# Attention, gated convolution and mixer in one kernel: four operand tiles instead of two for the eight heads scored in fp32, loaded two heads ahead

## The chip, the cores and the metric

The kernel runs on one core of a Trainium2 chip. The metric is the device time of one execution in microseconds (us). A core has a matrix engine (TensorE, PE in the profile), three engines for elementwise work (VectorE, DVE; ScalarE, ACT; GpSimd, POOL) and a queue engine (SyncE, SP) that does little but issue DMA transfers. Each engine runs its own instructions in program order; semaphores make one wait for another. ACT can issue DMAs too, and here it issues a handful at the start.

## What is computed

Three stages follow each other: attention with a bias that decays along the sequence, a gated convolution block, and a mixer.

```python
# attention: batch 4, 8 heads, 576 positions, 64 values per head
scores = scale * np.matmul(q, k.transpose(0, 1, 3, 2))
cum = np.cumsum(np.maximum(s, 0.0), axis=-1)
bias = -(cum[:, :, :, None] - cum[:, :, None, :])
scores = np.where(causal, -1000000000.0, scores + np.minimum(bias, 0.0))
attn = softmax(scores)
x = np.matmul(attn, v)             # heads side by side: 512 values per position
# gated convolution: 512 -> 1024 -> 512
h = np.maximum(x @ w_in, 0.0)
conv_out = sum of h shifted by -1, 0, 1 times conv_w
x = h * sigmoid(conv_out) @ w_out
# mixer
u = x + mixing over positions by U @ V (rank 32)
out = u + np.maximum(u @ w_ch1, 0.0) @ w_ch2
```

## The kernel before, in words

**Attention.** There are 32 heads (4 batches of 8), taken one after the other by `att_head`, in pairs for the last rows and for the products with v. For a head, PE makes the scores in blocks of 128 query rows (`scores`, L693: blocks of 128, 256, 384 and 512 columns, named sc0 to sc3 behind the head's number) and, for a pair of heads, the last 64 rows of both (`scores4`, L709). DVE takes the maximum of each block with the mask (L654), ACT takes the exponentials into tiles P (L671), POOL multiplies them by the reciprocal of the row sums (L682), PE transposes them by a multiplication with `ident` (`transp`, L816, into pt), ACT copies the result to tiles th (L357), and PE multiplies those with v (`av`, L842). As each pair is done, ACT and POOL split its output x into a high and a low part (xh, xl), which the first product of the gated block (`m1_in`, L886, into h) takes. Those products do not hang on later heads, so they serve PE as work to fill in with.

**The eight fp32 heads.** The 24 later heads take their scores from operands that are split into two rounded parts (qkA and qkB). The first eight heads, `FS = range(8)`, take them in fp32 from one operand tile qkF: partitions 64 to 127 hold the head's q and k (288 KB from memory, L592), partitions 0 and 1 hold a row of ones or minus ones and the head's row of the running sum cc (2.2 KB each), and the rest of partitions 0 to 63 is zero. There are two such tiles, qkF_0 for even heads and qkF_1 for odd ones. DVE clears their lower half once (L455) and ACT issues the four DMAs of ones (L458). `prep4(h)` (L588 to L601) issues the head's q and k (L592) and the two rows of cc (L594 and L599; for heads 0 and 1 the second goes through ACT, L597). Heads 0 and 1 are loaded at the start; from head 2 on, `att_head(h)` asks for head h + 1. The tile is in use until the scores of the head two before, with the pair's last rows, are done. The two tiles are then taken over by qkA of heads 8 and 9, as they are two buffers of the same ring, "qkA".

**What else goes on in this stretch.** The weights of the gated block (w1, 16 pieces of 512 KB, L539) are loaded through two buffers and decoded by ACT (L513) and DVE (L520, L529), then rounded by ACT (L357) and reduced to the rest by DVE (L366). The first eight pieces belong to heads 0 to 7 and go to tiles w1h and w1l. The other eight go to the tile `ws` of 8192 columns, under the name w1o; before that, `ws` holds early data: the rounded cc in columns 0 to 1151 (rk) and the raw mask in columns 1152 to 1343.

**What sets the order.** The kernel records all its operations with a cost each, and a planner (`Plan.order`) then lists them for each engine: at each point it takes, of the operations whose inputs are ready by its costs, the one that was recorded first. An earlier load therefore changes the order on all engines. All loads stand in SP's one queue; an instruction there that waits holds up all behind it. Eight semaphores are handed out to the DMAs in turn, those that ACT issues included, so that a DMA is issued only after the DMA eight places before it in the plan's order has landed.

Of the kernel before, what the change touches and what calls it, by code (L numbers as in the profile page):

```python
# [8 lines left out]
F32 = mybir.dt.float32  # L9
# [9 lines left out]
B, H, S, D = 4, 8, 576, 64  # L19
# [8 lines left out]
FS = range(8)  # L28
# [26 lines left out]
def f32(ap):  # L55
    return ap.bitcast(F32)
# [256 lines left out]
def tile_attention_moe_mixer(  # L313
# [14 lines left out]
    nc = tc.nc  # L328
    plan = Plan(tc)


    def dve(n, fn, r, w, fast=False):
        far = st.get("late") and any(getattr(x, "pool", None) is banks for x in r)
        return plan.op("DVE", (155 if far else 70) + n * (0.52 if fast else 1.042), fn, r, w)
# [4 lines left out]
    def pool(n, fn, r, w, two=False, extra=125):  # L339
        return plan.op("POOL", ((280 if st.get("late") else 148) + n * 2.1) if two else (37 + n * 0.834 + extra), fn, r, w)  # L340

    def dma(nbytes, fn, r, w):
        return plan.op("SP", 640, fn, r, w, late=nbytes / 360)

    def dma_act(fn, r, w):

        return plan.op("ACT", 100, fn, r, w, late=1900)
# [24 lines left out]
    st = {}  # L372
# [12 lines left out]
    def ring(pool_, cls, count, shape, dtype, name, at={}):  # L385
        n = at[pool_, cls] = at.get((pool_, cls), -1) + 1
        return pool_.buf(f"{cls}{n % count}", shape, dtype, name)
# [17 lines left out]
    def one(pool_, name, shape, dtype):  # L405
        return pool_.buf(name, shape, dtype, name)
# [8 lines left out]
    def early(name, at, shape, dtype, rows=128):  # L415
        n = 1
        for x in shape:
            n *= x
        axes = " ".join("abc"[: len(shape)])

        def view(t):
            v = t[:rows, at : at + n]
            if dtype != F32:
                v = v.bitcast(dtype)
            return v.rearrange(f"p ({axes}) -> p {axes}", **dict(zip("abc", shape)))

        return Part(ws, view, name)
# [13 lines left out]
    sm4s = [one(ap, f"sm4_{i}", [128, 5], F32) for i in range(2)]  # L441


    cc = one(ap, "cc", [NH, S], F32)
    rk = early("rk", 0, (2, S), F32R, NH)
    qkFs = [ring(ap, "qkA", RINGS["qk"], [128, 2, S], F32, f"qkF_{i}") for i in range(2)]

    def cum():
        return cc()
# [14 lines left out]
    scan = dve(S, lambda: nc.vector.tensor_tensor_scan(cum(), cum(), cum(), 0.0, ALU.add, ALU.max), key, key)  # L464

    def behind(o, back=1):
        o.preds.add([x for x in plan.ops if x.eng == "PE"][-back])
# [20 lines left out]
    def clear(t):  # L488

        o = pool(2 * S, lambda: nc.gpsimd.memset(f32(t[0:64]), 0.0), [], [(t, "r"), (t, "q")], extra=0)  # L490
        behind(o)

    for t in p4s:
        o = pool(64, lambda t=t: nc.gpsimd.memset(t[:, S:640], 0.0), [], [(t, "pad")], extra=0)
# [88 lines left out]
    def p_tiles(g):  # L583
        return [ring(ap, f"P{i}_", RINGS["P"], [128, 128 * (i + 1)], F32, f"P{g}_{i}") for i in range(4)] + [
            p4s[g // 2 % 2]
        ]

    def prep4(h):  # L588

        t = qkFs[h % 2]  # L590
        a = slice(64 * (h % 2), 64 * (h % 2) + 64)
        dma(294912, lambda: nc.sync.dma_start(out=t[64:128], in_=qk[h // 2, a]), [], [(t, "q")])  # L592
        rows = dma(
            2304, lambda: nc.sync.dma_start(out=t[0:1, 1, :], in_=cum()[h : h + 1]), [cc], [(t, "r0")]  # L594
        )
        if h < 2:
            dma_act(lambda: nc.scalar.dma_start(out=t[1:2, 0, :], in_=cum()[h : h + 1]), [cc], [(t, "r1")])  # L597
        else:
            dma(2304, lambda: nc.sync.dma_start(out=t[1:2, 0, :], in_=cum()[h : h + 1]), [cc], [(t, "r1")])  # L599
        st.setdefault("first", rows)  # L600
        st[h] = dict(qk=[t], P=p_tiles(h), sm=sms[h % 2])  # L601

    def prep_v(h):

        vr = ring(ap, "vr", RINGS["vr"], [128, 2, 5, 64], F32, f"vr{h}")
        dma(327680, lambda: nc.sync.dma_start(out=vr(), in_=vP[h // 2]), [], [vr]).preds.add(st["first"])
        st["v", h // 2] = vr

    def prep(h):

        t1 = ring(ap, "t1", RINGS["qkh"], [128, 2, S], F32R, f"t1_{h}")
        t2 = ring(ap, "t2", RINGS["qkh"], [128, 2, S], F32R, f"t2_{h}")

        for c, (hi, lo) in enumerate(((t1, t2), (t2, t1))):

            def raw(c=c, lo=lo):
                return f32(lo[:, c, :])

            dma(294912, lambda c=c, raw=raw: nc.sync.dma_start(out=raw(), in_=qk[h // 2, :, c]), [], [(lo, c)]).slack = WIRE
            if h == len(FS):  # L620
                behind(plan.ops[-1], 25)
            hi_pool(lambda c=c, hi=hi: hi[:, c, :], raw, [(lo, c)], [(hi, c)], S)
            lo_dve(
                lambda c=c, lo=lo: lo[:, c, :],
                raw,
                lambda c=c, hi=hi: hi[:, c, :],
                [(lo, c), (hi, c)],
                [(lo, c)],
                S,
            )  # L630
        st["pair", h // 2] = (t1, t2)
# [676 lines left out]


    prep4(0)  # L1310
    prep4(1)
    prep_v(0)
    mraw = early("mraw", 2 * S, (192,), F32)
    dma(98304, lambda: nc.sync.dma_start(out=mraw(), in_=mask_d), [], [mraw])
    for c, n in ((0, 384), (512, 224)):
        o = pool(n, lambda c=c, n=n: nc.gpsimd.memset(mask[:, c : c + n], 0.0), [], [(mask, c)], extra=0)
# [17 lines left out]
    def att_head(h):  # L1334

        if h + 1 < NH:
            if h % 2 == 1:
                prep_v(h + 1)
            if h + 1 in FS:
                if h:  # L1340
                    prep4(h + 1)
            else:
                if h % 2 == 1:
                    prep(h + 1)
                place(h + 1)
        if h == 3:
            decay_parts()
            for t in qkBs:
                clear(t)
        for i in range(2):  # L1350
            if h < NH:
                scores(h, i)
        if h > 0:
            transp(h - 1, 0)
        if h < NH:
            scores(h, 2)
        if h > 0:
            transp(h - 1, 1)
            if h % 2 == 0:
                av(h - 2, 0)  # L1360
        if h < NH:
            scores(h, 3)
        if h > 0:
            transp(h - 1, 2)
            transp(h - 1, 3)
        if h < NH and h % 2 == 0:
            scores4(h)
        if h > 0 and h % 2 == 0:
            av(h - 2, 1)
# [133 lines left out]
    for g in range(2):  # L1503
        blk = (w2a, u1p)[g].buf(f"u{g}", [128, 2 * 7 * S], F32R, f"w2_{g}")
        for i in range(7):
            f = 7 * g + i
# [89 lines left out]
```

## Time and profile before

| what | value |
|---|---|
| time, median of 3 runs (lowest to highest) | 809.51 us (807.74 to 813.28) |
| time of the profiled execution | 810.78 us |
| span of the profiled execution, first to last instruction | 809.0 us |
| PE busy | 788.1 us (97%), 5300 instructions |
| DVE, ACT, POOL busy | 477.1 us (59%), 465.8 us (58%), 181.5 us (22%) |
| TensorE clock granted, mean | 0.998 of full speed |

How to read it: an engine's busy share is taken over the whole span, and this kernel has stages of different kinds. In the forty slices of the profile's page, PE stands at 5, 8 and 8 tenths in the first three (20 us each), where the eight fp32 heads are, and at 9 from the fourth on except for the last. The rows below are from that part, up to about 90 us, and from the summary of the rest.

### The profile page before, as it was taken

The page shows a single profiled execution, that of the slowest core. Times are in us where ns is not written, and L with a number is a line of the kernel's source. Part 1 is how long each engine was busy: PE and PEld are TensorE (multiplying, and loading weights), DVE is VectorE, ACT ScalarE, POOL GpSimd, SP SyncE. Part 2 cuts the span into 40 slices and gives each one's busy share as a digit, 9 for nine tenths or more (in the row PEclk, how much of TensorE's full clock was granted, in tenths as well). Part 3 has the DMA queues.
Part 4 walks back from the last instruction along what each step waited for, and adds up shares of the span by engine and source line. Part 5 has one row for each costly group of instructions (what it writes and reads, how often), then busy time and mean ns, then how long its engine had stood idle before and what let it go on. Part 6 is the DMA issues. An engine that isn't in the chain of part 4 may idle for free.

```text
span 809.0 us, 15163 instructions
## 1 busy us (share of the span) xinstructions
PE 788.1 (97%) x5300; PEld 707.1 (87%) x5300; DVE 477.1 (59%) x1152; ACT 465.8 (58%) x1176; POOL 181.5 (22%) x291
## 2 busy tenths in 40 slices
PE   5889999999999999999999999999999999999998
PEld 3557798999899998999999999999998888888888
DVE  5977897636855368547888967444566232323232
ACT  4878898858868488776767545444455222222221
POOL 2554464634446245241220000000000000000000
PEclk9999999999999999999999999999999999999999
DMA  6578655554454456130226356455588363636343
GB/s 166 176 207 227 188 142 151 138 135 106 149 136 108 105 131 188 35 111 1 103 68 225 121 162 210 148 180 183 168 261 275 92 207 92 204 96 191 110 130 93
DMA packets 66309, 119.69 MB, mean 148 GB/s; under 512 B 9396, under 2 KB 34868, under 8 KB 66232
## 3 DMA queue, kind: packets, MB, share of 16 engines
q1 hardware_dynamic: 66160, 118.70, 50.7%
q8 instruction: 42, 0.69, 0.3%
q14 instruction: 35, 0.29, 0.1%
q10 hardware_dynamic: 72, 0.01, 0.0%
HBM read 68.81 MB, written 28.90 MB: 121 GB/s over the span
## 4 chain that ended last, share of the span: by engine, by line
PE 88%; DVE 4%; ACT 3%; DMA 2%; issue 1%; POOL 0%; SPq 0%; DVEq 0%; POOLq 0%
PE my L1273 24%; PE ma_A L1173 16%; PE y L928 12%; PE h L886 11%; PE ma_S L1173 6%; PE sc L693 6%; PE pt L816 5%; PE av L842 5%; DMA qkA<-t 1%; PE tp L945 1%; PE t L964 1%; DVE sc L654 1%; DMA qkF<-cc 1%; PE mh L991 1%; DVE wf_w L529 1%
## 5 line engine op out<-in xcount | busy, mean ns | idle before, releaser
L1273 PE MATMUL my<-mh,w 128*128 128x512 f32 (+1 forms) x560 | 159.1, 368 | 0.0
L1173 PE MATMUL ma_A<-u,W 128*128 128x288 f32 x960 | 137.9, 295 | 0.0
L1173 PEld LDWEIGHTS ma_A<-u,W 128*128 128x128 f32 x960 | 131.4, 188 | 0.3
L1251 ACT ACTIVATE mh<-ml 128x512 fp32r<-128x512 f32 (+1 forms) x80 | 47.1, 589 | 136.8 <-DMA ml<-ch_d 76.0
L1273 PEld LDWEIGHTS my<-mh,w 128*128 128x128 f32 x560 | 101.6, 189 | 17.6
L1254 DVE SCALAR_TENSOR_TENSOR ml<-ml,mh 128x512 fp32r<-128x512 f32 (+1 forms) x80 | 50.5, 638 | 112.6 <-ACT mh L1251 112.6
L928 PE MATMUL y<-gh,w1o 128*128 128x288 f32 x512 | 113.9, 299 | 0.1
L1273 PE MATMUL my<-ml,w 128*128 128x512 f32 (+1 forms) x280 | 103.0, 368 | 0.0
L682 POOL TENSOR_SCALAR P<-P,sm 128x128 f32<-128x128 f32 (+3 forms) x128 | 73.2, 591 | 101.3 <-DVE sm L745 86.5
L654 DVE CUSTOM_DVE_ANT_0 sc<-sc,mask 128x128 f32<-128x128 f32 (+2 forms) x144 | 69.2, 497 | 33.8 <-PE sc L693 26.1
L928 PEld LDWEIGHTS y<-gh,w1o 128*128 128x128 f32 x512 | 85.4, 188 | 0.9 <-DVE c L907 0.3
L898 DVE SCALAR_TENSOR_TENSOR c<-h,cw,c 128x288 f32<-128x288 f32 x128 | 64.3, 512 | 30.9 <-ACT c L894 29.8
L886 PE MATMUL h<-xh,w1h 128*128 128x290 f32 x256 | 79.9, 312 | 0.1
L369 POOL TENSOR_TENSOR gl<-c,gh 128x288 fp32r<-128x288 f32 x64 | 53.7, 846 | 104.0 <-ACT gh L913 89.2
L886 PE MATMUL h<-xl,w1h 128*128 128x290 f32 x256 | 76.6, 299 | 0.0
L886 PE MATMUL h<-xh,w1l 128*128 128x290 f32 x256 | 76.4, 298 | 0.0
L1187 ACT COPY s<-ma_A 128x288 f32<-128x288 f32 x96 | 38.3, 401 | 64.7 <-PE ma_A L1173 56.1
L928 PE MATMUL y<-gl,w1o 128*128 128x288 f32 x256 | 75.2, 294 | 0.0
L671 ACT ACTIVATE P<-sc,sm 128x128 f32<-128x128 f32 (+3 forms) x128 | 67.8, 533 | 5.9 <-DVE sm L654 5.4
L357 ACT COPY th<-pt 128x384 f32<-128x384 f32 (+2 forms) x128 | 63.1, 494 | 9.9 <-PE pt L816 9.0
L816 PE MATMUL pt<-ident,P 128*128 128x128 f32 x320 | 59.7, 274 | 2.3 <-ACT h L892 1.3
L1273 PEld LDWEIGHTS my<-ml,w 128*128 128x128 f32 x280 | 52.8, 189 | 8.6
(135 smaller groups left out, 1527.8 us busy)
## 6 DMA issues: line engine op xcount, KB each, us to landing
ml<-ch_d SPq DMA_DIRECT2D x64, 256.0 KB
ch_d<-s SPq DMA_DIRECT2D x64, 144.0 KB
raw_w<-w_in SPq DMA_DIRECT2D x16, 512.0 KB
raw_w2a<-w_in SPq DMA_DIRECT2D x16, 512.0 KB
raw_w2b<-w_in SPq DMA_DIRECT2D x16, 512.0 KB
t<-qk_in SPq DMA_DIRECT2D x24, 288.0 KB
qkB<-t SPq DMA_DIRECT2D x24, 288.0 KB
qkA<-t SPq DMA_DIRECT2D x24, 288.0 KB
```

Source lines behind the costliest of these rows:

```text
L357: act(n, lambda: nc.scalar.copy(out(), src()), r, w)
L369: pool(n, lambda: nc.gpsimd.tensor_tensor(out(), src(), f32(hi()), ALU.subtract), r, w, two=True)
L654: lambda: nc.vector.tensor_tensor_reduce(out=ps[:rows, :w], in0=ps[:rows, :w], in1=mask[:rows, m0 : m0 + w], scale=-0.125, scalar=3.0e38 i ...
L671: lambda: nc.scalar.activation(out(), ps[:rows, :w], ACTF.Exp, bias=low(), scale=-1.0, accum_out=total()),
L682: lambda: nc.gpsimd.tensor_scalar(t[:, :w], t[:, :w], r(), 1.0, ALU.mult, ALU.mult),
L816: nc.tensor.transpose(pt[:, o + rows - 128 : o + rows], d["P"][i][:, 128 * j : 128 * j + 128], turn)
L886: nc.tensor.matmul(ps[:, :W], lhsT=ww, rhs=xx, start=kt + n == 0, stop=kt == KT - 1 and n == 2)
L898: lambda k=k: nc.vector.scalar_tensor_tensor(c(), hh[:, k : k + HS], cw[:, 3 * f + k : 3 * f + k + 1], c(), ALU.mult, ALU.add),
L928: nc.tensor.matmul(ps[:, :HS], lhsT=ww, rhs=xx(), start=f + n == 0, stop=f == NF1 - 1 and n == 2)
L1173: nc.tensor.matmul(ps[:, :HS], lhsT=ww, rhs=uu, start=first and k == 0, stop=k == 5, skip_group_check=True)
L1254: lambda: nc.vector.scalar_tensor_tensor(ml[:, :n], raw(), 0.0, f32(mh[:, :n]), ALU.max, ALU.subtract),
L1273: nc.tensor.matmul(ys[c][dt][:, :n], lhsT=ww, rhs=xx[:, :n], start=f + k == 0, stop=f == NF2 - 1 and k == 2)
```

## The change

Two more operand tiles, qkF_2 and qkF_3, are laid into columns 2048 to 3199 and 3200 to 4351 of `ws`, which has no other user there until w1o is written. Their lower halves are cleared by POOL (1152 columns of 64 partitions each), and their four rows of ones are loaded by four more DMAs in SP's queue, which the planner may place only after the first head's row of cc. `prep4(h)` takes tile h % 4. `att_head(h)` now asks for head h + 2, so heads 2 and 3 are asked for when head 0 and head 1 begin. Head 4 goes into qkF_0 again, head 7 into qkF_3. The last users of qkF_0 and qkF_1 are now heads 4 and 5, and w1o may be written only after the scores of heads 6 and 7.

```diff
--- before.py
+++ after.py
@@ -441,6 +441,7 @@
     sm4s = [one(ap, f"sm4_{i}", [128, 5], F32) for i in range(2)]
 
 
+    rows4 = []
     cc = one(ap, "cc", [NH, S], F32)
     rk = early("rk", 0, (2, S), F32R, NH)
     qkFs = [ring(ap, "qkA", RINGS["qk"], [128, 2, S], F32, f"qkF_{i}") for i in range(2)]
@@ -489,6 +490,17 @@
 
         o = pool(2 * S, lambda: nc.gpsimd.memset(f32(t[0:64]), 0.0), [], [(t, "r"), (t, "q")], extra=0)
         behind(o)
+
+    for n in range(2):
+        t = early(f"qkF_{2 + n}", 2048 + n * 2 * S, (2, S), F32)
+        low = early(f"qkF_{2 + n}z", 2048 + n * 2 * S, (2, S), F32, 64)
+        low.state = t.state
+        o = pool(2 * S, lambda low=low: nc.gpsimd.memset(low(), 0.0), [], [(t, "z"), (t, "r0"), (t, "r1")], extra=0)
+        o.preds.add(scan)
+        for i in range(2):
+            dma(2304, lambda t=t, i=i: nc.sync.dma_start(out=t[i : i + 1, i, :], in_=one_d[i, 0:1, 0, :]), [], [(t, "z")])
+            rows4.append(plan.ops[-1])
+        qkFs.append(t)
 
     for t in p4s:
         o = pool(64, lambda t=t: nc.gpsimd.memset(t[:, S:640], 0.0), [], [(t, "pad")], extra=0)
@@ -587,7 +599,7 @@
 
     def prep4(h):
 
-        t = qkFs[h % 2]
+        t = qkFs[h % 4]
         a = slice(64 * (h % 2), 64 * (h % 2) + 64)
         dma(294912, lambda: nc.sync.dma_start(out=t[64:128], in_=qk[h // 2, a]), [], [(t, "q")])
         rows = dma(
@@ -597,7 +609,10 @@
             dma_act(lambda: nc.scalar.dma_start(out=t[1:2, 0, :], in_=cum()[h : h + 1]), [cc], [(t, "r1")])
         else:
             dma(2304, lambda: nc.sync.dma_start(out=t[1:2, 0, :], in_=cum()[h : h + 1]), [cc], [(t, "r1")])
-        st.setdefault("first", rows)
+        if "first" not in st:
+            st["first"] = rows
+            for o in rows4:
+                o.preds.add(rows)
         st[h] = dict(qk=[t], P=p_tiles(h), sm=sms[h % 2])
 
     def prep_v(h):
@@ -1336,10 +1351,9 @@
         if h + 1 < NH:
             if h % 2 == 1:
                 prep_v(h + 1)
-            if h + 1 in FS:
-                if h:
-                    prep4(h + 1)
-            else:
+            if h + 2 in FS:
+                prep4(h + 2)
+            if h + 1 not in FS:
                 if h % 2 == 1:
                     prep(h + 1)
                 place(h + 1)
```

The planner makes another order of this for the first 580 or so of PE's 3842 rows, and the same one behind that. Three places, as the built programs have them. In the names, the last number only counts buffers; P0_1 is block 1 of head 0, pt0_1 its second group of transposes, sc2_0 the first block of scores of head 2; all of rk, the mask and the new operand tiles carry the name ws. Lines are those of each program.

SP's queue at the start, up to the first load of v, before:

```order
L451 DMA cc_108<-s_in 32x576
L592 DMA qkF_0_104<-qk_in 64x1152
L592 DMA qkF_1_129<-qk_in 64x1152
L1314 DMA ws_134<-mask_in 128x192
L594 DMA qkF_0_104<-cc_108 1x16x36
L594 DMA qkF_1_129<-cc_108 1x16x36
L606 DMA vr0_155<-vP_in 128x640
```

and of the change:

```order
L452 DMA cc_108<-s_in 32x576
L604 DMA qkF_0_104<-qk_in 64x1152
L604 DMA qkF_1_129<-qk_in 64x1152
L1329 DMA ws_134<-mask_in 128x192
L604 DMA ws_134<-qk_in 64x1152 x2
L606 DMA qkF_0_104<-cc_108 1x16x36
L606 DMA qkF_1_129<-cc_108 1x16x36
L606 DMA ws_134<-cc_108 1x16x36
L611 DMA ws_134<-cc_108 1x16x36
L606 DMA ws_134<-cc_108 1x16x36
L501 DMA ws_134<-one_in 1x576 x2
L621 DMA vr0_178<-vP_in 128x640
```

The q and k of heads 2 and 3 moved ahead of the rows of heads 0 and 1. By the eight semaphores, the second of them (head 3) is issued after the second of ACT's rows of ones has landed, and the row of head 0 behind it after q and k of head 1 have landed. Behind the rows of heads 0 and 1 stand five more small loads before the first v.

On PE, three blocks of head 2's scores (sc2_0 to sc2_2) moved from behind the second group of head 0's transposes (pt0_1) to ahead of it.

ACT's rows around its rounding of the fourth piece of w1 (w1h_3), before:

```order
L671 ACTIVATE P3_2_431,sm_1_199<-sc3_2_405,sm_1_199 128x384
L357 CAST w1h_3_440<-wf_w1_3_0_409 128x512
L357 COPY th2_2_446<-pt2_2_433 128x384
L671 ACTIVATE P3_3_451,sm_1_199<-sc3_3_423,sm_1_199 128x512
L357 COPY th2_3_462<-pt2_3_453 128x320
```

and of the change:

```order
L686 ACTIVATE P3_2_447,sm_1_202<-sc3_2_408,sm_1_202 128x384
L357 COPY th2_2_453<-pt2_2_439 128x384
L686 ACTIVATE P3_3_461,sm_1_202<-sc3_3_428,sm_1_202 128x512
L357 COPY th2_3_468<-pt2_3_455 128x320
L686 ACTIVATE P4_0_476,sm_0_164<-sc4_0_445,sm_0_164 128x128
L357 CAST w1h_3_482<-wf_w1_3_0_459 128x512
```

The rounding moved behind two copies of head 2's transposes and the first exponential of head 4.

SP's queue around the load of head 7, before:

```order
L539 DMA raw_w1_7_0_597<-w1_in 128x512
L606 DMA vr6_604<-vP_in 128x640
L539 DMA raw_w1_0_512_632<-w1_in 128x512
L592 DMA qkF_1_129<-qk_in 64x1152
L594 DMA qkF_1_129<-cc_108 1x16x36
L599 DMA qkF_1_129<-cc_108 1x16x36
```

and of the change:

```order
L551 DMA raw_w1_4_0_433<-w1_in 128x512
L477 DMA r_d_57<-ws_134 64x1x576 x2
L604 DMA ws_134<-qk_in 64x1152
L606 DMA ws_134<-cc_108 1x16x36
L611 DMA ws_134<-cc_108 1x16x36
L551 DMA raw_w1_5_0_492<-w1_in 128x512
```

Head 7's load moved from behind the ninth piece of w1 to behind the fifth.

## Rows read from the trace of the kernel before

**Rows 1.** Busy time by stretch: us, length, engines' busy time (instructions), PEclk, DMA, GB/s

```profile
10.00:92.00 82.00, 72.56 (x445) 47.54 (x444) 64.48 (x185) 68.18 (x192) 42.12 (x59) 0.98 0.72 203
92.00:200.00 108.00, 107.79 (x821) 97.67 (x820) 72.38 (x216) 85.98 (x249) 53.42 (x84) 1.00 0.56 138
200.00:700.00 500.00, 499.73 (x3480) 468.86 (x3479) 303.31 (x688) 285.93 (x692) 84.63 (x131) 1.00 0.48 145
```

**Rows 2.** Waits of PE in 0 to 120 us: us in total, times, longest

```profile
PE sc L693 <- DMA qkF<-cc: 7.5, 1, 7.5
PE sc L709 <- DMA qkF<-cc: 2.2, 1, 2.2
PE sc L693 <- ACT th L357: 1.5, 1, 1.5
PE pt L816 <- ACT h L892: 1.3, 1, 1.3
...
PE sc L693 <- DMA qkA<-t: 0.4, 1, 0.4
```

**Rows 3.** Timeline of the start: start us, us, engine, line, operation

```profile
1.19 1.21 SPq L592 DMA_DIRECT2D qkF<-qk_in  x2
1.20 0.64 POOL L1316 MEMSET mask<- 128x384 bf16 x2
...
2.44 0.58 SPq L1314 DMA_DIRECT2D ws<-mask_in  x1
...
4.98 1.22 SPq L594 DMA_DIRECT2D qkF<-cc  x2
...
6.55 0.35 SPq L606 DMA_DIRECT2D vr<-vP_in  x1
...
7.47 2.26 PE L693 MATMUL sc<-qkF 128*128 128x128 f32 x5 [7.47 <-DMA qkF<-cc]
```

**Rows 4.** Instructions on tile qkF in 0 to 7.6 us: duration min/median/max, first and last start

```profile
L458 ACTq DMA_DIRECT2D qkF<-one_in x4: 213/264/513, 2.1 to 3.8; - x4
...
L597 ACTq DMA_DIRECT2D qkF<-cc x2: 504/556/607, 5.3 to 6.6; - x2
```

**Rows 5.** Busy time by stretch, columns as in rows 1

```profile
2.00:6.00 4.00, 0.00 (x0) 0.00 (x0) 2.73 (x4) 0.00 (x0) 0.00 (x0) 1.00 0.80 184
86.90:90.40 3.50, 3.50 (x18) 2.46 (x16) 2.02 (x5) 3.14 (x9) 1.66 (x3) 0.51 1.04 241
7.50:11.90 4.40, 4.40 (x8) 2.21 (x8) 1.47 (x6) 2.58 (x7) 0.00 (x0) 1.00 0.84 231
```

**Rows 6.** Timeline of PE, 17 to 20 us

```profile
17.46 0.33 PE L816 MATMUL pt<-ident,p 128*128 128x128 f32 x1 [0.72 <-POOL p L682]
...
19.41 1.24 PE L693 MATMUL sc<-qkF 128*128 128x256 f32 x4
```

**Rows 7.** Timelines of PE, DVE and ACT around 57 us, with the idle time before

```profile
56.85 0.67 PE L709 MATMUL sc<-qkF 128*64 128x288 f32 x2 [2.24 <-DMA qkF<-cc]
...
57.56 0.47 DVE L654 CUSTOM_DVE_ANT_0 sc<-sc,mask 128x288 f32<-128x288 f32 x1 [2.55 <-PE sc L709]
...
58.26 0.59 ACT L357 COPY th<-pt 128x512 f32<-128x512 f32 x1 [2.31 <-PE pt L816]
```

**Rows 8.** Timelines of DVE and POOL, 26 to 34 us

```profile
26.83 0.86 DVE L529 SCALAR_TENSOR_TENSOR wf_w<-raw_w,wf_w 128x512 int32<-128x512 int32 x1
...
31.30 2.65 DVE L529 SCALAR_TENSOR_TENSOR wf_w<-raw_w,wf_w 128x512 int32<-128x512 int32 x1
...
32.20 1.20 POOL L369 TENSOR_TENSOR xl<-x,xh 128x576 fp32r<-128x576 f32 x1
```

**Rows 9.** Instructions on tile qkB in 25 to 40 us: duration, starts

```profile
L490 POOL MEMSET qkB<- x2: 1050/1188/1327, 29.9 to 31.2; 64x1152 f32 x2
```

**Rows 10.** First rounding into w1o (timeline of ACT), first product from it (timeline of PE)

```profile
73.52 0.62 ACT L357 CAST w1o<-wf_w 128x512 fp32r<-128x512 f32 x1
...
112.96 0.40 PE L928 MATMUL y<-gh,w1o 128*128 128x288 f32 x1
```

## The prediction

> **What bounds the kernel now.** I read the busy time by stretch first, then PE's waits, then the timelines at the places that they name. Behind 92 us PE is the bound: in the 608 us from 92 to 700 it is idle for 0.5 us [rows 1]. The order of the instructions is the same there with the change, so whatever PE gains or loses up to 92 us should reach the end unchanged. Ahead of that lie three things a load could touch: the start, where PE waits 7.47 us for the first head's row of cc [rows 2, 3]; the idle time from 10 to 92 us, 82.00 - 72.56 = 9.44 us [rows 1]; and a stretch of 3.5 us at a granted clock of 0.51, which is the lower of the two levels and costs 3.5 x 0.49 = 1.7 us [rows 5]. All that could ever be won is therefore 9.44 + 1.7 = 11.1 us of some 810, and the start can only get worse.
>
> Of the 9.44 us, little waits for an operand tile. The list of PE's waits has one of 2.2 us for a row of cc in a qkF tile, and one of 0.4 us for a qkA tile, which takes its place over from a qkF tile [rows 2]. The first is the load of head 7. It cannot start before qkF_1 is free, and it then stands behind big pieces of w1. At 56.85 us DVE had been idle for 2.55 us and ACT for 2.31 us until PE went on [rows 7], so no other engine would have held PE up in its place. The rest waits for ACT, DVE and POOL.
>
> **The change, term by term.**
>
> *The start: loss.* SP now issues q and k of heads 2 and 3 ahead of head 0's row. Head 2's fits into SP's gap, which runs from 3.02 (the end of the mask's issue) to 4.98 us [rows 3]. Head 3's must wait for ACT's second row of ones to land. When does that land? ACT's second issue of a cc row waits for the same row of ones: the two issues are 0.5 to 0.6 us each, yet the second starts at 6.6 us, over a microsecond after the first at 5.3 [rows 4]. So it lands at about 6.55 us. Head 3's issue takes 1.21 / 2 = 0.6 us, so head 0's row is issued at about 7.15 instead of 4.98 us: +2.2 us. By another way: the two loads are 590 KB more on the wire ahead of that row; at the 231 GB/s that the busy stretch behind the start shows [rows 5] that is 2.55 us. The two ways overlap and do not add; I take **+2.4 us**. The least is +1.6 us: the row also waits for head 1's q and k, as the first load of v does now, which starts at 6.55 us behind a gap of 0.35 us [rows 3], and 6.55 - 4.98 = 1.57. The most is +4.0 us: if the row of ones lands behind head 2's data too, 295 KB at the 184 GB/s of 2 to 6 us [rows 5] are 1.6 us more on top of 2.4.
>
> *Other work added at the start: nothing.* POOL clears two lower halves, 1.05 to 1.33 us each by the same clear of the qkB tiles [rows 9]. Its clear of the mask moves from 1.20 to about 3.6 us [rows 3], while DVE needs it only behind the first scores, at 8 us or later. In SP's queue three more rows of cc (0.61 us each) and two rows of ones (up to 0.51 us each, by those on ACT [rows 4]) stand ahead of the first v, which moves from 6.55 to about 7.15 + 5 x 0.61 + 2 x 0.51 = 11.2 us; `ident` comes about 0.4 us behind it, and two more rows of ones stand behind that. A load takes about 2.5 us from its issue until PE goes on (4.98 to 7.47 [rows 3]), so `ident` is there at 14 us. The first transposes stand just ahead of 17.46 us [rows 6] and move back with the start. Were that cover gone, PE would stand still at the transposes for as long as it is short. The writes to w1o now wait for heads 6 and 7 as well; the first is at 73.5 us and the first use of w1o at 113.0 us [rows 10], 39 us apart, so this costs nothing.
>
> *Filling the pipeline: gain.* PE waits 0.72 us for POOL's first big product at 17.46 us [rows 6]. Three blocks of head 2's scores now stand ahead of that place, and two blocks of such scores alone are 1.24 us [rows 6]. **-0.7 us** (0 at worst, if these blocks wait for ACT to free their PSUM banks).
>
> *Head 7's wait: gain.* Its load now stands behind the fifth piece of w1 instead of the ninth, and its tile is free when head 3 is done, not when head 5 is. **-2.2 us**, from rows 7, and 0 only if another wait stood there.
>
> *The qkA wait: gain.* qkF_0 and qkF_1 are done with at heads 4 and 5, two heads earlier. **-0.4 us** [rows 2].
>
> *Waits for ACT, DVE and POOL: open.* What is left is 9.44 - 0.72 - 2.24 - 0.4 = 6.1 us. The largest, 1.5 us for ACT's copy th [rows 2], comes from an accident: DVE's step of the w1 decode at 31.30 us takes 2.65 us where it took 0.86 us shortly before, beside a POOL instruction that ends at 33.40 us [rows 8], and ACT's rounding of that piece stands ahead of the copy. In the changed order ACT's rounding of that piece stands behind the copies, so I take this 1.5 us as gone. For the other 4.6 us no row says how they change. All of it could go, since scores two heads ahead give the softmax more time. Or it could grow by a new wait as long as the longest in the list, 2.2 us, since ACT is busy for 68.18 of the 82 us and PE now gets to it sooner [rows 1]. I take -1.0 us, nearer to no change: earlier loads shorten no work of ACT. Together **-2.5 us**, between -6.1 and +2.2.
>
> *The clock.* The stretch at the lower level begins behind idle times of PE in 84 to 87 us, one of them the 1.3 us for ACT [rows 2]. If these close, 1.7 us come back; if another such cluster appears, 1.7 us go. I take 0.
>
> *Sum:* +2.4 - 0.7 - 2.2 - 0.4 - 2.5 = **-3.4 us**. The profiled execution took 810.78 us, 1.8 us of it around its span of 809.0, so it would take 807.4 us. The median of the three runs is 1.27 us below the profiled execution, and I predict against the median: 809.51 - 3.4 = **806 us**.
>
> [...] The row of ones that ACT issued at 3.3 us or a little later took until 6.55 us to land, by the start of ACT's next issue [rows 4]. [...]
>
> **The rivals.**
>
> 1. *No net gain, because the engines take over.* Without DMA waits PE gets to ACT, DVE and POOL sooner and waits there. Then the three sure gains (3.3 us) are won, the 6.1 us stay, and one of the gains is given back as a new wait: +2.4 - 3.3 = -0.9 us, up to +1.3 us. The time is 808.6 to 810.8 us. ACT's 83% of busy time in this stretch speaks for it [rows 1]; its idle time at 57 us speaks against it [rows 7]. Here belongs also the case that the change does not do what it says, because a load asked for two heads ahead sits in SP's queue behind a piece of w1 that waits for its buffer.
>
> 2. *Slower: the start costs more than everything else gives.* The mechanism is the chain of waits in SP's queue: ones row, then head 3's q and k, then head 0's row. It costs +4.0 us if the ones row lands late; with only the sure 3.3 us won and one new wait of 2.2 us for ACT it is +2.9 us, 812.4 us. The point from which it decides is PE's first score: if it starts later than 7.47 + 3.3 = 10.8 us, the loads won are already spent. Against it: head 0's row only needs what was issued by 7 us, and the wire is not idle meanwhile.
>
> 3. *The large gain.* All 6.1 us of the waits go and the clock stays up: +2.4 - 3.3 - 6.1 - 1.7 = -8.7 us, 800.8 us. Against it: seven or more separate causes would have to go at once.
>
> **Chances.** The forecast, -1.5 to -7 us, 0.55; rival 1 0.27; rival 2 0.12; rival 3 0.06. The range of 802 to 812 us leaves out the large gain and the worse half of rival 2, and about 0.1 for the scatter of the runs, which is 5.5 us among the three of before: 0.8 are left. A measurement of this kernel can tell about 1% from no change, that is 8.1 us. Faster by over 1% (below 801.4 us) is rival 3, 0.06; slower by over 1% (above 817.6 us) needs more than every upper end together, 0.02; the rest, 0.92, is within 1%.
>
> **What the profile will show.** PE's first score at 9.7 to 10.0 us (11.4 us in rival 2). No wait of PE for a DMA into ws or qkF but the first, and none for qkA8 or qkA9. No wait of 0.7 us for POOL at the first transposes. Idle time from 10 to 92 us of about 4 us plus what of the start falls behind 10 us, instead of 9.4; if it is still 6 us or more and ACT ends it, rival 1 is right. A stretch of half clock of some 3.4 us somewhere, or none. Behind 92 us, nothing. The prediction is wrong if the first score starts before 9 or after 11 us, if a load of a later head still holds PE, or if time is lost behind 92 us, which no row leads me to expect.

## The result: 0.8% slower, and the profile after

The changed kernel takes 816.56 us in the median of nine runs (813.53 to 819.46), the kernel before on the same chip 809.83 us: the ratio is 1.0077, 95% interval 1.0056 to 1.0098, or some 6.2 us more (6.7 us between the two medians). The forecast of 806 us lay on the wrong side, and the range ended at 812. The profiled execution took 818.17 us, with a span of 816.4 us and a mean granted clock of 0.994. (Line numbers moved: scores L708, last rows L724, transposes L831, av L857, h L901, POOL's multiplication L697.)

Busy time by stretch, columns as in [rows 1]:

```profile
10.00:92.00 82.00, 70.40 (x428) 48.20 (x429) 59.10 (x177) 64.07 (x182) 38.72 (x56) 0.96 0.73 185
92.00:200.00 108.00, 106.61 (x805) 96.28 (x804) 74.71 (x217) 86.13 (x246) 54.75 (x83) 0.98 0.58 145
200.00:700.00 500.00, 498.63 (x3485) 467.81 (x3484) 302.20 (x692) 288.18 (x705) 87.10 (x134) 1.00 0.48 143
```

PE's idle time from 10 to 92 us is 11.60 us instead of 9.44; 0.64 of it belongs to the start, which now reaches behind 10 us. From 92 to 200 us it is 1.39 us, where 0.21 stood. What PE waits for from 0 to 120 us, to be held against [rows 2] (us in total, times, longest):

```profile
PE sc L708 <- DMA qkF<-cc: 10.6, 1, 10.6
PE sc L708 <- ACT th L357: 3.1, 2, 2.6
PE sc L708 <- issue: 3.0, 1, 3.0
PE pt L831 <- ACT th L357: 2.6, 1, 2.6
PE pt L831 <- POOL P L697: 1.4, 2, 0.9
```

The waits that the prediction called sure gains are gone: none for head 7's row, none for qkA, none for POOL at the first transposes. But the first score starts at 10.6 us instead of 7.5, and three waits stand there that are each longer than any behind the start of the kernel before: 2.63 us at 37, 3.04 us at 69 and 2.55 us at 92 us.

**The start.** Timeline of SP (3.06, 7.18), POOL (1.03) and PE, as in [rows 3]:

```profile
1.03 2.05 POOL L498 MEMSET ws<- 64x1152 f32 x2
...
3.06 4.00 SPq L604 DMA_DIRECT2D ws<-qk_in  x2
7.18 1.21 SPq L606 DMA_DIRECT2D qkF<-cc  x2
...
10.64 1.62 PE L708 MATMUL sc<-qkF 128*128 128x128 f32 x4 [10.64 <-DMA qkF<-cc]
```

Head 0's row leaves at 7.18 us instead of 4.98 (+2.20) and PE starts 3.46 us behind it instead of 2.49 (+0.97).

**The wait at 37 us.** Timelines of DVE, POOL, ACT and PE:

```profile
31.75 2.45 DVE L532 TENSOR_SCALAR wf_w<-raw_w 128x512 int32<-128x512 int32 x1 [1.02 <-ACT raw_w L525]
34.12 1.44 DVE L363 CAST ws<-cc 32x576 fp32r<-32x576 f32 x1
...
31.87 2.05 POOL L491 MEMSET qkB<- 64x1152 f32 x2
33.90 1.36 POOL L369 TENSOR_TENSOR xl<-x,xh 128x576 fp32r<-128x576 f32 x1
...
36.20 0.62 ACT L357 CAST w1h<-wf_w 128x512 fp32r<-128x512 f32 x1 [3.08 <-DVE wf_w L541]
36.73 0.58 ACT L357 COPY th<-pt 128x512 f32<-128x512 f32 x1
...
37.36 0.99 PE L708 MATMUL sc<-qkF 128*128 128x128 f32 x4 [2.63 <-ACT th L357]
```

DVE's step of the w1 decode begins with POOL's clear of the two qkB tiles and takes 2.45 us; the cast behind it takes 1.44 us beside POOL's xl. ACT has nothing to do for 3.08 us until the decode is done, and the copy th that PE needs stands behind that rounding.

**The wait at 69 us.** Timelines of SP and PE, then the busy time of 54 to 66 us:

```profile
52.03 3.01 SPq L656 DMA_DIRECT2D qkA<-t  x4
56.10 0.34 SPq L551 DMA_DIRECT2D raw_w<-w_in  x1
57.35 1.21 SPq L656 DMA_DIRECT2D qkA<-t  x2
59.58 1.10 SPq L656 DMA_DIRECT2D qkB<-t  x2
...
68.96 0.44 PE L708 MATMUL sc<-qkB 128*128 128x128 f32 x1 [3.04 <-issue]
```

```profile
62.00:66.00 4.00, 3.92 (x29) 2.07 (x27) 2.76 (x9) 3.31 (x10) 1.00 (x2) 1.00 1.03 182
54.00:62.00 8.00, 6.43 (x41) 3.71 (x40) 7.66 (x26) 6.75 (x21) 6.14 (x8) 1.00 1.02 199
```

As qkF_0 and qkF_1 are free two heads earlier, the copies that build qkA and qkB of heads 8 and 9 are all sent from 52 to 61 us, with pieces of w1 between, and the DMA engines' busy share is 1.02 and 1.03 in the two rows above. PE needs qkB of head 8 first; it stands behind six copies into qkA. The profile names nothing that ends this wait ("issue"); that it is this copy rests on the run with head 8's copies first, below.

**The wait at 92 us.** Timelines of ACT and PE:

```profile
88.55 0.67 ACT L525 ACTIVATE raw_w<-raw_w 128x512 f32<-128x512 f32 x1 [0.64 <-DMA raw_w<-w_in]
...
89.89 0.62 ACT L357 CAST w1o<-wf_w 128x512 fp32r<-128x512 f32 x1
...
91.07 0.49 ACT L357 COPY th<-pt 128x384 f32<-128x384 f32 x1
...
91.61 0.33 PE L831 MATMUL pt<-ident,p 128*128 128x128 f32 x1 [2.55 <-ACT th L357]
```

ACT waits 0.64 us for a late piece of w1, and the decode and a rounding stand ahead of the copy.

**The clock.** With each of these three waits goes a stretch at the lower of the two clock levels that the traces show (granted clock 0.50; outside such stretches it is 1.00 in this execution and in that of [rows 5]), which begins 0.15 us ahead of the end of the second wait and 0.7 and 1.1 us behind the ends of the other two. The kernel before had one such stretch [rows 5]. While it lasts PE works at about half speed: in the last one, products h start 0.24 us apart instead of 0.13 (timeline of PE):

```profile
38.08:41.49 3.41, 3.41 (x10) 2.33 (x9) 3.27 (x13) 3.41 (x12) 1.11 (x2) 0.50 0.85 260
...
68.81:72.22 3.41, 3.26 (x15) 3.19 (x16) 1.29 (x6) 1.30 (x4) 1.98 (x4) 0.50 0.95 313
92.70:96.10 3.40, 3.40 (x17) 2.74 (x17) 3.02 (x9) 2.50 (x7) 1.78 (x2) 0.50 0.60 142
```

```profile
92.49 0.29 PE L901 MATMUL h<-xl,w1h 128*128 128x290 f32 x1
92.62 0.36 PE L901 MATMUL h<-xh,w1l 128*128 128x290 f32 x1
...
93.26 0.44 PE L901 MATMUL h<-xh,w1l 128*128 128x290 f32 x1
93.50 0.45 PE L901 MATMUL h<-xh,w1h 128*128 128x290 f32 x1
```

One such stretch costs 3.41 x (1 - 0.13 / 0.24) = 1.6 us.

### The profile page after: what moved, and what is told of

Read it like the earlier page. It is cut to its first block, busy times and chain, and to the rows that moved or that the text cites. A ratio compares the mean times of both kernels' runs of the same rounds, so it can differ in the third digit from the quotient of the medians.

```text
span 816.4 us, 15166 instructions
## 1 busy us (share of the span) xinstructions
PE 788.4 (97%) x5300; PEld 709.4 (87%) x5300; DVE 477.1 (58%) x1152; ACT 465.1 (57%) x1176; POOL 184.2 (23%) x293
## 4 chain that ended last, share of the span: by engine, by line
PE 84%; ACT 5%; DMA 4%; DVE 4%; issue 1%; SPq 0%; POOL 0%; DVEq 0%; ACTq 0%
PE my L1288 24%; PE ma_A L1188 14%; PE y L943 12%; PE h L901 10%; PE sc L708 6%; PE ma_S L1188 6%; PE pt L831 5%; PE av L857 4%; DMA raw_w<-w_in 2%; DMA raw_w2b<-w_in 2%; PE tp L960 1%; PE t L979 1%; ACT P L686 1%; ACT th L357 1%; DVE c L913 1%
## 5 line engine op out<-in xcount | busy, mean ns | idle before, releaser
L697 POOL TENSOR_SCALAR P<-P,sm 128x128 f32<-128x128 f32 (+3 forms) x128 | 75.4, 607 | 107.8 <-DVE sm L760 85.6
L901 PE MATMUL h<-xh,w1h 128*128 128x290 f32 x256 | 80.1, 313 | 0.0
L901 PE MATMUL h<-xh,w1l 128*128 128x290 f32 x256 | 76.9, 300 | 0.0
L901 PE MATMUL h<-xl,w1h 128*128 128x290 f32 x256 | 76.9, 300 | 0.0
L357 ACT COPY th<-pt 128x384 f32<-128x384 f32 (+2 forms) x128 | 63.5, 496 | 10.6 <-PE pt L831 9.7
L831 PE MATMUL pt<-ident,P 128*128 128x128 f32 x320 | 60.3, 276 | 1.8 <-POOL P L697 1.8
```

The lines of the kernel that those rows point to most:

```text
L357: act(n, lambda: nc.scalar.copy(out(), src()), r, w)
L697: lambda: nc.gpsimd.tensor_scalar(t[:, :w], t[:, :w], r(), 1.0, ALU.mult, ALU.mult),
L831: nc.tensor.transpose(pt[:, o + rows - 128 : o + rows], d["P"][i][:, 128 * j : 128 * j + 128], turn)
L901: nc.tensor.matmul(ps[:, :W], lhsT=ww, rhs=xx, start=kt + n == 0, stop=kt == KT - 1 and n == 2)
```

## The experiments

Two theories stood against each other. By the first the loss is the start. By the second it is the new order on all engines that the planner makes for earlier loads, with its waits. Each kernel below is the changed one with one edit, or the kernel before where that is said.

**Rows first.** q and k of heads 2 and 3 go behind the rows of heads 0 and 1; the planner then makes another order.

```diff
+        if h in (2, 3):
+            plan.ops[-1].preds.add(st["second"])   # the row of head 1
```

> The change, with one thing undone: q and k of heads 2 and 3 may be issued only behind the cc rows of heads 0 and 1. Theory: the start is lost by SP's order alone (head 3's load waits for a row of ones, and head 0's row stands behind it). PE's first score then goes back from 10.64 to 7.5-8.2 us and the kernel gains 2.4 to 3.2 us on the changed one (about 813.5 us). Rival: the stretch up to 137 us is bound by ACT and DVE, so an earlier start is given back in later waits; the first score is early but the time stays within 1 us of 816.6. No theory of the start touches PE's waits at 37, 69 and 92 us.

Measured: 809.70 us, ratio to the kernel before 1.0002 (0.9991 to 1.0013); first score at 7.54 us. More came back than the start's 3.17 us: the long waits and the half-clock stretches are gone too (mean clock 1.0 in the profiled execution), and the longest wait behind the start is 1.3 us:

```profile
PE pt L835 <- ACT th L357: 2.5, 2, 1.3
```

In this order, loads two heads ahead gain nothing even where they cost nothing at the start.

**Order held, only SP's queue changed.** The same move, made behind the planner, so that PE, ACT, DVE and POOL keep the changed kernel's order.

```diff
-            for o in self.order():
+            ops = [o for o in self.order() if o not in self.late]   # late: q, k of heads 2, 3
+            n = ops.index(self.second) + 1
+            for o in ops[:n] + self.late + ops[n:]:
                 o.fn()
```

> The changed kernel with every engine's instructions in exactly its order, PE, ACT, DVE and POOL included; only in SP's queue q and k of heads 2 and 3 stand behind the rows of heads 0 and 1 instead of ahead of them. The rows-first run had this too, but the planner then made another order for all engines. Theory A, the order: POOL's clear beside DVE, the bunched copies of heads 8 and 9 and ACT's late rounding lie in the order, so the three waits of 2.5 to 3 us and the half-clock stretches stay, PE's first score is at 7.5 us, and the end comes 2 to 3.5 us earlier than the changed kernel's 816.56: 813 to 814.5 us (ratio about 1.005). Theory B, the timing: the waits come because the engines run late against the loads of w1, and with the start back they go: 809 to 811 us (1.000 to 1.002).

Measured: 813.52 us, ratio 1.0044 (1.0026 to 1.0061). PE's waits, columns as above:

```profile
PE sc L715 <- DMA qkF<-cc: 7.5, 1, 7.5
PE sc L715 <- ACT th L360: 3.1, 2, 2.6
PE sc L715 <- issue: 2.8, 1, 2.8
PE pt L838 <- ACT th L360: 2.7, 2, 1.8
```

The start is back, the waits at 37, 69 and 92 us (now 2.62, 2.78 and 1.82 us) stay, the third one shorter and without its half-clock stretch: behind it products h start 0.13 us apart, where they are 0.24 us apart behind the first (37.18 and 37.42 us). Theory A holds in the main: the waits lie in the order, and only the third is longer with the late start. The order alone costs 0.0044 x 810 = 3.6 us, give or take 1.4; the start costs 0.0077 - 0.0044 = 0.0033, or 2.7 us, give or take 2.2, as both intervals enter.

**Rows first, with a late start.** Two loads that nothing reads are put where the change has those of heads 2 and 3.

```diff
+    for n in range(2):
+        t = early(f"extra_{n}", 4352 + n * 2 * S, (2, S), F32)
+        dma(294912, lambda t=t, n=n: nc.sync.dma_start(out=t[64:128], in_=qk[1, 64 * n : 64 * n + 64]), [], [(t, "q")])
```

> Rows first (809.70 us, loads two heads ahead, its own order on all engines) with two loads of 288 KB that nothing reads sent ahead of the first row of cc, so that PE starts late as in the changed kernel; order of all engines as in rows first but for one ACT and one DVE instruction moved by two places. Theory A, the order: this order has no long waits, so the late start costs what it costs in the kernel before, the first score is at 10.7 us and the end at 811 to 813 us (ratio 1.002 to 1.004). Theory B, the timing: the late start itself makes the long waits and the half-clock stretches of the changed kernel, 815 to 817 us.

Measured: 812.33 us, 1.0034 (1.0020 to 1.0047), first score at 10.57 us. Against rows first that is 0.0032, 2.6 us, give or take 1.4: the price of the start a second time, in another order. The time speaks for theory A, but not purely. In the profiled execution, which at 814.41 us was 2.1 us above the median, one wait of 1.12 us had grown to 2.12, and two half-clock stretches stood in it (products h 0.24 us apart at 39 and at 106 us, mean clock 0.996). Of the nine runs five show a mean clock of 1.0 and four 0.996 to 0.999; rows first has 0.998 in two of ten and 1.0 in the others. So such stretches come in this order too, though not in every run, and the lowest clocks with the late start.

**The kernel before, with a late start.** The same two loads in the kernel before (columns from 2048); its order is unchanged on every engine.

> The kernel before with one addition: SP sends two loads of 288 KB into columns of ws that nothing reads, at the place where the change sends q and k of heads 2 and 3; order on every engine as before. This is the price of the start alone. Theory: PE's first score at about 10.6 us (+3.2), nothing of it is caught up, since PE's order is unchanged, the waits behind it keep their size, and the end comes 3 to 3.5 us later (ratio about 1.004). Rival: the later start changes which data arrive in time, new waits of 1 to 3 us come as in the changed kernel, and the end comes 5 to 7 us later (1.006 to 1.009); or the waits at 17, 35 and 57 us soak it up and the end comes under 2 us later.

Measured: 811.42 us, 1.0003 (0.9988 to 1.0019). PE's waits:

```profile
PE sc L693 <- DMA qkF<-cc: 10.8, 1, 10.8
...
PE sc L709 <- DMA qkF<-cc: 0.3, 1, 0.3
```

PE runs 3.3 us late up to 55 us, and then head 7's wait is 0.29 us instead of 2.24, there is none for qkA, and no half-clock stretch comes (mean clock 1.0 in all ten runs). Here most of the late start was taken up (it cost 0.2 us, at most 1.5 by the interval), which the expectation had only as a rival. The missing half-clock stretches pay for a part: on this chip the kernel before had 0.6 of them a run (mean clock 0.9987), or some 1.0 us. What paid for the rest in most runs is not shown.

**The kernel before, with the clear early.** POOL clears the qkB tiles at the start; the order is otherwise unchanged.

```diff
-        behind(o)                 # in clear(t), called at head 3
+        o.preds.add(scan)         # called at the start
```

> The kernel before with one edit: POOL clears the lower halves of the two qkB tiles at the start instead of at head 3; every other instruction keeps its place. Theory: DVE's step of the w1 decode at 31.3 us took 2.65 us because POOL was clearing qkB beside it, and PE's 1.53 us wait at 35 us follows from it. Then the step takes about 0.9 us, the wait goes to under 0.3 us, and the end comes 1 to 1.5 us earlier (ratio 0.998 to 0.999). Rival: another wait takes its place behind it and the end moves by less than 0.5 us.

Measured: 810.40 us, 1.0002 (0.9978 to 1.0025). The interval holds theory and rival alike. DVE's step of [rows 8] takes 1.64 us instead of 2.65, and the wait for th 0.52 instead of 1.53 (timelines of POOL, DVE and PE):

```profile
31.42 1.67 POOL L369 TENSOR_TENSOR xl<-x,xh 128x576 fp32r<-128x576 f32 x1 [0.76 <-ACT xh L357]
32.00 1.64 DVE L529 SCALAR_TENSOR_TENSOR wf_w<-raw_w,wf_w 128x512 int32<-128x512 int32 x1
...
54.59 0.67 PE L709 MATMUL sc<-qkF 128*64 128x288 f32 x2 [0.29 <-DMA qkF<-cc]
```

But the step ends 0.55 us behind the end of POOL's xl in both kernels (33.64 and 33.09 us here, 33.95 and 33.40 in [rows 8]), so in the kernel before it is xl that it ends with, and the clear does little more than push xl back. The step ends only 0.3 us earlier here; it is 1.0 us shorter because it also starts 0.7 us later, and PE too arrives 0.7 us later at its wait for th (34.19 us instead of 33.50).

Head 7's wait is 0.29 us here as well. SP issued head 7's second row 0.33 us earlier than in the kernel before, and PE took it 2.26 us earlier. So two kernels with the old order and two tiles do not have the 2.24 us on which the largest sure gain rested.

**The early clear in the changed kernel.**

> The change, with POOL's two clears of the qkB tiles moved from behind head 2's last normalisation (about 32 us) to the start. Theory: PE's wait of 2.63 us at 37.36 us comes from POOL's clear holding back a DVE step of the w1 decode (2.45 us instead of 0.43), behind which ACT's rounding and the copy th stand; with the clear gone that DVE step takes 0.4 to 0.6 us, the wait falls below 0.8 us, the half clock behind it goes too, and the kernel gains 2.6 to 4.3 us on the changed one (812.3 to 814 us). Rival: ACT has too much to do there; the wait stays over 1.5 us and the gain under 1 us.

Measured: 814.65 us, 1.0055 (1.0036 to 1.0073). Without the clear beside them the two DVE steps take 0.48 and 0.43 us (timeline of DVE):

```profile
31.58 0.48 DVE L532 TENSOR_SCALAR wf_w<-raw_w 128x512 int32<-128x512 int32 x1 [0.99 <-ACT raw_w L525]
31.98 0.43 DVE L363 CAST ws<-cc 32x576 fp32r<-32x576 f32 x1
```

The wait at 37 us is gone, and PE, ACT and DVE keep the changed kernel's order here, so POOL's clear was its cause. The wait for head 8's copy (2.92 us, now ending at 66 us) stays, with a half-clock stretch twice as long around its end (65.22 to 72.05 us at a granted clock of 0.50), and so does one of 2.23 us at 90 us.

**Head 8's copies first in the changed kernel.**

```diff
+            if g == 8:
+                st.setdefault("eighth", []).append(o)
+            if g == 9:
+                o.preds.update(st["eighth"])
```

> The change, with the copies of head 9's operands kept behind those of head 8 (before, the ring's tile enforced this). Theory: PE's wait of 3.04 us at 68.96 us is the early freeing of both qkF tiles: ten copies of two heads are then sent in one go with pieces of w1 between, the DMA engines are full from 54 to 70 us, and the one copy that head 8 needs lands last. With head 8 first its copy lands 2.5 to 3.4 us earlier, the wait falls below 0.8 us and its half clock goes: 3 to 4.7 us gained on the changed one (812 to 813.6 us). Rival: the queue is full whatever the order; the wait moves to head 9's scores or to a w1 piece, and under 1 us is gained.

Measured: 815.09 us, 1.0067 (1.0052 to 1.0082). The wait at 69 us is gone, so the order of the copies was its cause; less purely shown than for the clear, as the planner changes PE's order too, from 68 us on. The wait at 92 us is gone as well. But up to 120 us PE now waits 4.1 us for POOL, where the changed kernel had 1.4, and once 1.8 us for DVE:

```profile
PE pt L836 <- POOL P L702: 4.1, 4, 1.5
PE sc L713 <- ACT th L357: 3.1, 2, 2.6
PE h L906 <- DVE c L927: 1.8, 1, 1.8
```

**Both of these edits.**

> The changed kernel with both order edits (POOL's clear of qkB at the start, head 9's copies behind head 8's) and with the late start left as the change has it. The queue-only run (ratio 1.0044) puts the order's share at about 3.5 us, and rows first late (1.0034) the start's share at about 2.7 us. Theory: the two edits take away the waits at 37 and 69 us, so only the start's share is left: first score at 10.6 us, 812.5 to 813.5 us, ratio 1.003 to 1.004. Rival: other waits of 1 to 2 us take their places, as in the run with head 8 first, and it stands at 814 to 815 us (1.005 to 1.006).

Measured: 814.32 us, 1.0064 (1.0045 to 1.0083). The rival is right. Neither long wait is left, but waits of 1.47, 1.53, 0.98 and 1.81 us stand behind them, and two half-clock stretches follow (second block, columns as in [rows 1]):

```profile
83.14 0.55 PE L836 MATMUL pt<-ident,P 128*128 128x128 f32 x3 [1.47 <-ACT w1o L357]
85.32 0.33 PE L836 MATMUL pt<-ident,P 128*128 128x128 f32 x1 [1.53 <-POOL P L702]
86.96 0.40 PE L906 MATMUL h<-xh,w1h 128*128 128x290 f32 x1 [0.98 <-ACT th L357]
...
106.34 0.40 PE L906 MATMUL h<-xh,w1h 128*128 128x290 f32 x1 [1.81 <-DVE c L927]
```

```profile
87.27:90.68 3.41, 3.41 (x17) 3.41 (x16) 1.73 (x7) 2.46 (x7) 1.56 (x2) 0.50 0.95 290
107.75:111.16 3.41, 3.41 (x17) 3.40 (x16) 3.41 (x11) 3.09 (x10) 0.80 (x1) 0.50 0.92 193
```

Against the changed kernel's 1.0077 the last three runs gain 1.8, 0.8 and 1.1 us, and none of these is clear of the noise of some 2 us. So the causes of two single waits are shown, but taking them away does not bring back the 3.6 us that the order costs: other waits and stretches come in their place. Only another order, as in rows first, did that.

**Only head 3 held back.** As rows first, for h == 3 alone.

> The changed kernel with only head 3's q and k held behind the rows of cc of heads 0 and 1; head 2's are sent early, as in the change. It splits the 3.17 us of the start. Theory of the queue: head 3's issue, which waits for ACT's second row of ones, is what holds SP up, so the first score is at 8 to 8.6 us (+0.6 to +1.1 us for 288 KB more on the wire). Rival, the wire: each of the two loads costs half, and the first score is at about 9.1 us (+1.6). End: 810 to 813 us.

Measured: 810.99 us, 1.0004 (0.9986 to 1.0023), first score at 9.25 us. The rival's time is right, but the halves are not alike. Timeline of SP:

```profile
3.06 0.47 SPq L604 DMA_DIRECT2D ws<-qk_in  x1
7.06 1.22 SPq L608 DMA_DIRECT2D qkF<-cc  x2
```

With one load ahead of it head 0's row leaves at 7.06 us, hardly earlier than with two, and PE starts 2.19 us behind it. So the first load makes the row leave 2.1 us late, which I put down to the slow row of ones, for which SP waits 3.1 us in the changed kernel; and the second one delays its landing by 3.46 - 2.19 = 1.3 us, as much as 295 KB at the 231 GB/s of [rows 5].

**All three edits** (rows first, early clear, head 8 first), run on two chips, and **rows first with the early clear**:

> The three edits together on the changed kernel. Theory: they are independent losses: first score at 7.5-8.2 us, none of the waits at 37 and 69 us, at most one half-clock stretch: 816.6 - 3 - 2.6 - 3 - 3.4 = 804.6 us, which is 5 us below the kernel before. Rival: the stretch is bound by ACT and DVE, so that the gains do not add: 808 to 811 us, no better than before.

Measured: 807.78 us, 0.9979 (0.9969 to 0.9988).

> All three edits again (rows first, early clear, head 8 first), which took 807.78 us against 809.55 before. Theory: the difference is the kernel's, ratio 0.997 to 0.999. Rival: it was the scatter of that chip, ratio 0.999 to 1.001.

Measured: 808.38 us, 0.9984 (0.9974 to 0.9995). This version beats both kernels, the kernel before by 1.3 to 1.7 us; 0.2% is all that four tiles with these edits gave here.

> The changed kernel with the rows of heads 0 and 1 ahead of q and k of heads 2 and 3 and with POOL's clear of qkB at the start, but without the edit on head 8's copies. With rows first alone (809.70 us) no wait at 69 us was left, so the theory is that the copies' edit adds nothing: 807.5 to 808.5 us, as with all three edits. Rival: the gain of all three over rows first came from the copies, and this stands at 809 to 810 us.

Measured: 809.10 us, 0.9989 (0.9960 to 1.0018), which does not tell theory from rival.

## Why the prediction was wrong, step by step

**Where the 6.2 us come from** (0.0077 x 810). The start is 2.6 to 2.7 us, by two pairs of kernels, each uncertain by 1.4 to 2.2 us. It is no fixed price: in the old order the same late start cost 0.2 us. The order is 3.6 us, by the run in which only SP's queue was changed. Much of the latter is clock: over its nine runs the changed kernel's mean granted clock was 0.9953. A stretch of 3.41 us takes (3.41 / 2) / 816 = 0.0021 off, so these are 2.2 stretches a run; the kernel before had 0.3 to 0.7 (mean clocks 0.9993 to 0.9986 over 20 to 31 runs). That is 1.5 to 1.9 stretches more, at 1.6 us each 2.4 to 3.0 us. The run with the order held has the same mean clock (0.9955 over four runs) with the early start, so this loss goes with the order. It is not all: the one run of the changed kernel with a mean clock of 1.0 still took 813.53 us.

**The start, +2.4: mis-sized by 0.8.** The chain in SP's queue was right: head 0's row was forecast to leave at 7.15 us and left at 7.18. Wrong was the sentence "the two ways overlap and do not add". The landing came 0.97 us later on top of the issue, for which the run with only head 3 held back gives the reason. The worse case, +4.0 us for a row of ones that lands later behind head 2's data, did not come: head 3's load was sent at 6.6 us, where 6.55 was forecast.

**The border at 92 us: a premise that failed.** The prediction took the order of the instructions behind 92 us to be the same, and expected nothing there. By the names in the traces, PE's order differs in the first 737 of its 5300 instructions, which reach to 136 us in the changed kernel. Its idle time from 92 to 200 us is 1.39 us where 0.21 stood, and the third half-clock stretch begins at 92.7 us.

**Filling the pipeline, -0.7: right in this order.** The wait for POOL is gone. In rows first, whose order differs, 0.72 us stand there again.

**Head 7 and qkA, -2.2 and -0.4: right as waits, wrong as gains.** Both are gone as forecast. But head 7's wait is 0.29 us in two kernels with the old order, and the one for qkA is missing there. I took a wait from one execution as a property of the kernel, and set it against the median of runs. The profiled execution was 1.27 us above that median, and I saw it and did not ask which wait that was. That the 2.24 us are what was special in it is likely, not shown, as no second profile of the kernel before was taken.

**Waits for ACT, DVE and POOL, -2.5, between -6.1 and +2.2: the step that failed.** Two of its sentences are wrong. "In the changed order ACT's rounding of that piece stands behind the copies, so I take this 1.5 us as gone": the first half of the sentence came true, the conclusion did not, as the cause, POOL's work beside DVE's decode, stayed. POOL's clear and xl met the decode of the piece of w1 before, and another rounding stood ahead of another copy: 2.63 us instead of 1.53. And the upper bound was one new wait as long as the longest in the list. Three came, each longer. The one at 69 us has its cause in the change itself: tiles that are free earlier send all their next user's copies into the same 10 us, in the planner's order and not in the order in which PE needs them. The front part says that qkF_0 and qkF_1 are handed on to qkA of heads 8 and 9; I followed that only as far as a gain of 0.4 us.

**The clock, 0: failed with the waits.** The prediction had one more cluster at 1.7 us as a bound, but did not tie it to the new waits. The three waits of over 2.5 us each have a stretch at or behind their end, and so do three others of that length in the runs above (2.62 and 2.78 us with the order held, 2.92 with the early clear). With head 8's copies first, where one of 2.63 us stands, the mean clock from 10 to 92 us is 0.96, as in the changed kernel with two stretches there. Head 7's wait of 2.24 us [rows 7] had none (clock 1.00 up to 86.75 us), and for the one of 2.23 us with the early clear none is left: the mean clock is 0.995 there as with the order held and its two stretches, and the one of 6.83 us takes as much as those two. Length alone does not decide it: the stretch of [rows 5] stands behind shorter waits, and the kernel before with a late start has the same short waits (0.65, 1.31 and 0.57 us) without it.

**Rivals.** What came is nearest to rival 2, given 0.12: a late start and new waits for ACT. Its point of decision, a first score later than 10.8 us, was wrong: it was 10.6 us and the kernel slower, as that point was worked out with 3.3 us of gains as sure. The sign set for rival 1 came as well, idle time of over 6 us from 10 to 92 us that ACT ends: 11.60 - 0.64 = 11.0 us, 5.7 of them ended by ACT's copies. But rival 1 had one new wait, with the other waits unchanged. That the time would stay within 1%, given 0.92, came true.

**What stays open.** In the profiled executions the changed kernel is 7.4 us longer. The start (3.2), the idle time up to 200 us (1.5 + 1.2), that behind it (1.1) and two more half-clock stretches (3.1) make 10.1 us. PE's busy time is 788.4 us against 788.1, though those two stretches should have added 3.1 to it. So PE's work became some 3 us shorter elsewhere. With the order held PE is busy for 787.7 us in spite of two stretches, so the shortening goes with the new order; what makes it is not shown. Of the 7.4 us, 2.2 come only behind 500 us, where the order is unchanged. The two kernels with the old order lose 0.7 and 1.3 us there against the same profile, so part of it is scatter. What makes the wait at 92 us was not taken apart: it is gone with head 8's copies first, and 1.82 us with the early start.

## What to carry to other kernels

A wait in one profile is one draw: before it is booked as a gain, look for it in a second execution or in a kernel with the same order. A load that is asked for earlier moves more than itself. Follow who takes the freed buffer next, in which order those transfers are sent, and which small transfer stands behind the load in its queue. A long wait can cost twice: here six of the seven waits of over 2.5 us behind the start are seen to cost once as idle time and once as a stretch at half clock, some 1.6 us for one of 3.41 us. And a named cause is not yet the loss: here two long waits were taken away, and shorter ones took their place.

## What the runs showed of the hardware

A DVE instruction beside POOL's clear took about as long as if it had waited the clear out: the TENSOR_SCALAR of the w1 decode took 2.45 us in the changed kernel, close to the 0.48 us of the same step with the clear moved plus the 2.05 us of the two clears. The CAST behind it took 1.44 us instead of 0.43. By the trace DVE's step started 0.12 us ahead of the clear (31.75 and 31.87 us). What holds DVE there is not shown.

One load of 288 KB in the queue ahead of a row of 2.2 KB made that row leave 2.1 us late (7.06 instead of 4.98 us, with only head 3 held back), and with a second one PE started 3.46 instead of 2.19 us behind it, another 1.3 us. And the same row, issued in the same order, reached PE 5.8 us after its issue in one kernel (51.01 to 56.85 us) and 3.9 and 3.7 us in two others (50.68 to 54.59, 54.55 to 58.20).
